# A new table of turns for the opening of a one-core attention and MLP kernel, and thirteen wide operations on other engines

## The chip, the cores and the metric

The kernel runs on one core of one Trainium2 chip. The metric is device time of one execution in microseconds, smaller is better. It is compared by the median of several runs. All engines are fed from instruction lists that are fixed when the program is built: PE (TensorE) does matmuls and transposes, DVE (VectorE), ACT (ScalarE) and POOL (GpSimd) work on tiles, and SP (SyncE) issues transfers.

## The reference, cut to what matters

```
q, k, v: [8, 8, 576, 64] fp32     w_in: [512, 2048]     w_out: [2048, 512]
q_s = softmax(q, over the 64 dims);  k_s = softmax(k, over the 576 positions)
kv  = k_s^T v                      # one 64x64 matrix for each head
x   = q_s kv                       # then laid out as 4608 tokens x 512
g   = s * relu(x @ w_in)^2 + b
out = g @ w_out                    # [4608, 512]
```

## The kernel before, in words

Eight batches (blocks of 512 tokens, and the 64 left over of each batch apart) go through two matmuls with 16 slices of the hidden dimension. For each block `t = 16 * blk + f` is a step: `step(t)` multiplies the slice f of w_in with x (12 matmuls of 512 columns into the one PSUM bank "h"), takes relu on ACT, squares and scales on DVE, and adds the slice's product with w_out to the accumulators (12 matmuls more). fp32 accuracy comes from splitting every operand into a high and a low part and multiplying high by high, high by low and low by high, so each operand costs one copy (ACT) for its high part and one subtraction (DVE) for its low part.

All weights are converted once, in the opening, by `conv_w(f)`: six operations in turn, ACT, DVE, ACT, DVE, ACT, DVE (lines 307, 311, 314, 318, 323, 326), on both halves of a slice at once (128x1024) or, for the slices in HALVES, on w_in's half ("a") and w_out's half ("b") by themselves (128x512). The attention of the first two batches is made in the opening too. `k_stream(u)` (u = 0 to 3) transposes k on PE (line 440), takes the maximum on DVE (443), the exponential on ACT (448), transposes back on PE (453) and copies the result (455, operation 4, engine by KN_ON). `kv_stream(pr)` takes the scales on DVE (408, 409), makes kv on PE (402) and scales it on DVE (420). `q_stream(u)` (u = 0 to 7) has twelve operations: 0 maximum (519), 1 subtract (522, engine by SUB_ON), 2 a small memset (526), 3 exponential (528), 4 sum (531), 5 reciprocal (533), 6 multiply (538, engine by MUL_ON), 7 transposes on PE (543), 8 copy (546, engine by QF_ON), 9 the product with kv on PE (553), 10 and 11 x's high part (559, ACT) and low part (563, DVE). `q_left` (582 to 610) does the 64 tokens left over, `k_pair` the k of the second batch. Step 0 can begin only when x of a head pair is there, and step 1 only when relu of step 0 has emptied the bank "h" and w_in's slice 1 is converted. From step 80 on the kernel multiplies by a scheme with fewer products; nothing of that is touched.

The order of the work on each engine is written into the program by a planner, `Order.run`. It holds one stream per piece of work (`conv_w`, `step`, `q_stream` and so on). The string TURNS_TAKEN holds 3557 turns, two letters each, and each names the stream whose next operation is issued. So the string fixes the order of all five instruction lists; each engine then runs its own list in that order and waits, at its head, for what the head needs. The planner's own clock has one effect left on the program: where it believes that PE is idle, `idle` (1691) puts transposes of no use into PE's list (tile "unused") until step 0, so that PE does not rest.

Below, `conv2.4` is operation 4 (counted from 0) of slice 2's conversion, `conv0b` that of w_out's half of slice 0, `q2.9` operation 9 of q_stream(2), `k3.4` operation 4 of k_stream(3), `kv1.2` operation 2 of kv_stream(1), `step0.8` the relu of step 0 (its operations 0 to 7 are its first product, 8 to 11 relu, square, high and low part, 12 to 15 its second product).

Of the kernel before, what the change touches and what calls it, by code (L numbers as in the profile page):

```python
# [26 lines left out]
def attention_moe(ctx: ExitStack, tc: tile.TileContext, q, k, v, w_in, w_out, s, b, out):  # L27
    nc = tc.nc
    B, H, S, D = q.shape
    DM, FF = w_in.shape  # L30
    DO = w_out.shape[1]
    P = 128
# [12 lines left out]
    AHEAD = min(4, FIRST)  # L45
    PAIRS = tuple((a, a + 1) for a in range(FIRST, B, 2))
    STEPS_ON_ACT = (17, 25, 26, 27, 37, 38, 40, 46, 48, 52, 53, 54, 59, 65, 75, 79)
    KN_ON = ('ACT', 'DVE', 'ACT', 'DVE')
    QF_ON = ('DVE', 'ACT', 'ACT', 'ACT', 'ACT', 'ACT', 'ACT', 'DVE')
    WARM = 20  # L50
    BEGIN = (-7.9, -6.8, 2.8, 1.8, 0.8, -0.0, -1.7, -0.6, 2.0, -3.6, -0.1, -5.5)
    SUB_ON = ('D', 'D', 'P', 'P', 'D', 'D', 'D', 'P')
    MUL_ON = ('P', 'D', 'P', 'D', 'D', 'D', 'P', 'D')
    HALVES = (0, 6, 11, 12, 13, 15)
    DUE_L = (0.5, 10.0, 12.0, 17.5)
    QF_AT_KE = (3, 4, 6)
# [70 lines left out]
    class Op:  # L127
# [8 lines left out]

    LETTERS = "abcdefghijklmnopqrstuvwxyzABCDEFGHIJKLMNOPQRSTUVWXYZ0123456789"
    TURNS_TAKEN = (
        "aaaaababaaaaabaaabaWabaWabaQaWaWabaQaWaQabaWaXaWaQabaXaRaQaWauaRaXabaXaWabaRaXaba8aRaXabaXavabaRabauaSavabaua8avaSabauabaSaYaoauaSa8aYaZaTaS"
        "aqauaWaYaZaYaTaXaWaYaTaZbcaYaWaYaZa9aTaXaZbcaXaTawaZaYaZaXa9awaYaXawavaZbcaZa9adbcawavaYadaxaZavaeaYaxaeacaZbcaYawaZbcbcacayawbcbcaye1axbdbc"  # L140
        "bda4bcaxbda4aybdbcafaxafa4aybdbcbdbcaxagbdbcagaUbcbdbeaUaybebda4beazayapbeaAbda4e2a4bdazbea4bdaAazbdbeaAa4bfazbfbeaAbfa4ahaza4ahbfbea4aiaDaU"
        "azbeaibfbeaDaAbebfbeaDaAbgbfbgaDe3aBbgaCbfbgakaDaBbfakaCa1bgbfaDaBbfaCbfbgaEbhaBbgbhaCbgaBbhajaCbhajaBbgaCbhe4a1bgaFbha1bga1aEbgbha1biaEbhbi"
        "a1bia1aGbiaEa1bibhaUalbiaFbhalaGbibha0bibha0a1aUbibja0aEaUbjaFaEbjbjaGaUbiaFaJbibjbiaJaUambjbiaJamaGbkbjbkaUaJanbkaFbjanbaa5aJaFa5aGbkarbaaK"
        "babjaJbaa5bjaKataGbjaKbkbjaKaHblbkaKblaHbkaKe5blaHbkblaIaHbkblaIbkaHblaIbkaHblbkaIe6a0bmblaIbma0asa5aIbmaNa0a1a0aLa5bma1a5aNblbma5a1blbmaVa0"
        "bmblaVbmblaLa0bnbmaNa0aNaLbna0bnaMa0bnaNaLa5bmaMbnaNbma5aLa5bnaMbma5aLbmbnaMe7boaObnboaMaOaPboaMaOaPboa2aPaVaObnboaVbnboaPaVboa2bnaVa2bnboaV"
        "bpaOaPbpboaVaObpaVaPbpe8a2a3bobpa2a3bobpa2boa2bpboa3bqbpa3a2bpbqa3a2bqa3a3bqbpbqeQeQbpbqbpbqbpbqa3bbbqa3brbbcubrbbbbbrcva2cwbra2bqa2brcxbqbr"
        "a3brbqbrbqa3brbsa3bsa6bsa7bsdgbrbsdgbrbsbrePdgdQbrbsdgePbtdQeQbtbtbseQbtdgdRdgbsbtbsdRbta6bsa7bta6bsbtbua7btbua6a7a6bua7a6a7bua6a7bta6bubta7"
        "bua6btbudgbta6budQa6bvdQbvdQbvdQbvbubvdQbubvdQbubvbubwbvdgbwbwdgdsbwdsa6bvdtcza7bwdtbva7bwdRbvbwa7dRbveea7e9bwbxe9dRbxfhdRdQbxfhefcydRfhbxdR"
        "efcBfhbwefbxbwfhefbxbwefdSbxbwfhdSbxfhbyfabyfhcCbyfibyfifhfibxbyfibxfidQbybxfadQbybxcAdhdSbzbybzdRdhbzdSbzdhdSbydhbzfbdSfibyerbzfibydhbzdSdh"
        "byerbzbAdSerbAfibAererdibAfifjbzdibAbzfjbAbzfbdTbAbzcDfjdRdTbAbBdRbBdhbBfjdTdibBdSfjdibAdTbBfcbAbBfjdTbAdifjdTdibAbBfjbCbBesdTfjbCbBesfkbCes"  # L150
        "bCdTfkesbBdhesbCfcbBfkbCdhbBdufkdUbBbCdufkbDdUdifkdvbDbCdvbDdSbCbDfkcEdSbCbDfkbCdUfdflbCbDflfkbCdUbDbEfldUbDflegdUdTflbDbEcFegbEflegflbEdieg"
        "bDbEdUegbDdwbEbDfddwflbEdUbDdicGbFbEdxbFflfmbFdxdVbFfmdVfmetbFfebEetbFbEfmbFetbEbFetbEetfmbGcHfmdTbGfmbGdTbGdVehfebGdVdUeSbGbFdVeSbGehcJbFdV"
# [235 lines left out]
    def copier(eng):  # L388
        return nc.scalar.copy if eng == "ACT" else nc.vector.tensor_copy

    def wide_op(on, part=1.0):
        return (("DVEp", 0.03 + 0.7 * part), nc.vector) if on == "D" else (("POOL", 0.1 + 1.16 * part), nc.gpsimd)
# [39 lines left out]
    def k_stream(u):  # L432
# [19 lines left out]
        for n in range(NT):  # L452
            nc.tensor.transpose(kn[:, n * P:(n + 1) * P], early[:, n * P:(n + 1) * P], ident)
        yield Op(KN_ON[u], 0.62 if KN_ON[u] == "ACT" else 0.73, due, free=[tag], gives=[f"k{u}"])
        copier(KN_ON[u])(kt, kn[:, 0:NT * P].rearrange("p (n h d) -> p h n d", n=NT, h=2))

# [51 lines left out]
    def q_stream(u):  # L508
# [10 lines left out]
        nc.vector.tensor_reduce(out=qm, in_=qt, axis=AX.X, op=ALU.max)  # L519
        on, engine = wide_op(SUB_ON[u], wide_)  # L520
        yield Op(*on, due)
# [11 lines left out]
        nc.vector.reciprocal(qs, qs)  # L533
        on, engine = wide_op(MUL_ON[u], wide_)
        yield Op(*on, due)
# [6 lines left out]
        for n in range(m):  # L542
            nc.tensor.transpose(qT[:, n * P:(n + 1) * P], qn[:, n].rearrange("p h d -> p (h d)"), ident)
        yield Op(QF_ON[u], (0.55 if QF_ON[u] == "ACT" else 0.66) * SM / S, due, free=[tag])
        qf = early[:, 0:SM] if at == "ke" else early[:, NT * P:NT * P + SM]
        copier(QF_ON[u])(qf, qT[:, 0:SM])
        yield Op("PE", 1.0 * SM / S, due, needs=[f"kvf{pr}"] + before * (bb > 0), take=[tag], free=[at])
# [1211 lines left out]
```

## Time and profile before

| | |
|---|---|
| median of 3 runs | 828.17 us (827.79 to 828.49) |
| the profiled execution | 828.27 us, of which the span is 826.5 us |
| PE busy | 817.6 us, 99% of the span |
| DVE, ACT, POOL busy | 81%, 56%, 25% of the span |
| TensorE's granted clock | full in every slice |
| DMA | 165.64 MB, mean 200 GB/s |

Busy is the time in which an engine had an instruction of the program under way. PE's matmuls are pipelined and their ends are modelled, so that a long wait shows as idle time and a short one as a larger distance between the starts of two matmuls.

### The profile page before, as it was taken

How to read it: one execution, taken by the hardware profiler on the slowest of the kernel's cores; microseconds unless marked ns; L12 is line 12 of the kernel's file. 1: busy time of each engine (PE TensorE's matmuls, PEld its weight loads, DVE VectorE, ACT ScalarE, POOL GpSimd, SP SyncE). 2: the span in 40 equal slices, each digit the busy share in tenths (PEclk: the TensorE clock that was granted, in tenths of full speed). 3: DMA queues.
4: the chain of work that ended last, by engine and by line, in shares of the span. 5: the costliest groups of instructions: out<-in, count | busy, mean ns of one | idle time of the engine just before them, and what ended most of it. 6: DMA issues, size and time to landing. Idle time of an engine off the chain costs nothing.

```text
span 826.5 us, 12888 instructions
## 1 busy us (share of the span) xinstructions
PE 817.6 (99%) x4301; PEld 676.7 (82%) x4301; DVE 673.3 (81%) x1155; ACT 463.5 (56%) x768; POOL 205.3 (25%) x206
## 2 busy tenths in 40 slices
PE   8999999999999999999999999999999999999997
PEld 7688888888888888888888888888888888888886
DVE  6999956799899996978979978699969976656883
ACT  4999964356446455564556555545447644445650
POOL 3100012212212122222222322335342005353500
PEclk9999999999999999999999999999999999999999
DMA  9999523587867666866695754789889967666314
GB/s 267 319 375 318 164 70 110 151 228 191 218 179 198 168 170 205 214 177 144 203 241 163 242 149 149 231 264 283 276 253 325 251 156 214 203 182 187 90 18 73
DMA packets 217206, 165.64 MB, mean 200 GB/s; under 512 B 91444, under 2 KB 200500, under 8 KB 217140
## 3 DMA queue, kind: packets, MB, share of 16 engines
q1 hardware_dynamic: 212116, 163.83, 68.6%
q10 hardware_dynamic: 5024, 0.98, 0.6%
q8 instruction: 34, 0.56, 0.3%
q14 instruction: 32, 0.26, 0.1%
HBM read 112.85 MB, written 52.44 MB: 200 GB/s over the span
## 4 chain that ended last, share of the span: by engine, by line
PE 96%; DVE 2%; issue 1%; ACT 0%; POOL 0%; POOLq 0%; ACTq 0%
PE acc L1548 27%; PE h L1468 26%; PE bankU L1104 11%; PE overX L1195 8%; PE bankV L1104 8%; PE overY L1195 5%; PE overZ L1195 5%; PE xp L830 2%; PE kv L402 2%; PE kT L440 1%; PE xp L553 1%; PE unused L1702 0%; PE bankU L1195 0%; DVE low L318 0%; DVE st L311 0%
## 5 line engine op out<-in xcount | busy, mean ns | idle before, releaser
L1468 PE MATMUL h<-x,w 128*128 128x512 f32 x960 | 238.2, 392 | 1.3 <-ACT r L1500 0.8
L1468 PEld LDWEIGHTS h<-x,w 128*128 128x128 f32 x960 | 177.9, 188 | 38.8 <-ACT r L1500 1.3
L1548 PE MATMUL acc<-w,gh 128*128 128x512 f32 x640 | 199.2, 392 | 0.0
L1548 PEld LDWEIGHTS acc<-w,gh 128*128 128x128 f32 x640 | 118.1, 188 | 23.5
L1548 PE MATMUL acc<-w,gl 128*128 128x512 f32 x320 | 125.1, 391 | 0.1
L1500 ACT ACTIVATE r<-h 128x512 f32<-128x512 f32 x80 | 47.9, 599 | 94.7 <-PE h L1468 94.1
L1104 PE MATMUL bankU<-w,ring 128*128 128x512 f32 x378 | 95.9, 389 | 0.0
L1104 PEld LDWEIGHTS bankU<-w,ring 128*128 128x128 f32 x378 | 70.9, 188 | 14.7
L1548 PEld LDWEIGHTS acc<-w,gl 128*128 128x128 f32 x320 | 60.1, 188 | 14.2 <-DVE gl L1527 0.9
L1104 PE MATMUL bankV<-w,ring 128*128 128x512 f32 x282 | 71.5, 389 | 0.0
L759 POOL TENSOR_TENSOR qe<-qe,qr 128x640 f32<-128x640 f32 x24 | 33.2, 1384 | 127.8 <-DVE qr L755 66.7
L1104 PEld LDWEIGHTS bankV<-w,ring 128*128 128x128 f32 x282 | 52.9, 188 | 11.0
L1514 DVE SCALAR_TENSOR_TENSOR h<-h,sb,r 128x512 f32<-128x512 f32 x47 | 35.3, 752 | 18.3 <-ACT r L1500 18.0
L742 POOL TENSOR_TENSOR area<-area,qm 128x640 f32<-128x640 f32 x24 | 31.2, 1300 | 74.3 <-DVE qm L740 45.4
L1516 ACT ACTIVATE gh<-h,sb 128x512 fp32r<-128x512 f32 x47 | 32.4, 690 | 28.6 <-DVE h L1514 28.5
L1195 PE MATMUL overX<-w,w 128*128 128x512 f32 (+1 forms) x177 | 40.5, 384 | 0.0
L1195 PEld LDWEIGHTS overX<-w,w 128*128 128x128 f32 x177 | 32.7, 188 | 6.5
L1518 DVE SCALAR_TENSOR_TENSOR gl<-h,sb,gh 128x512 fp32r<-128x512 f32 x47 | 34.7, 738 | 3.4 <-ACT gh L1516 3.2
L1510 DVE TENSOR_TENSOR gl<-r,gh 128x512 fp32r<-128x512 f32 x23 | 17.5, 762 | 15.6 <-ACT gh L1508 15.5
L927 DVE TENSOR_TENSOR S<-S 128x128 f32<-128x128 f32 x64 | 26.7, 418 | 0.7
L1195 PE MATMUL overZ<-gh,w 128*128 128x512 f32 x88 | 27.1, 389 | 0.0
L927 DVE TENSOR_TENSOR Z<-Z 128x128 f32<-128x128 f32 x64 | 25.2, 394 | 1.0
(329 smaller groups left out, 1524.1 us busy)
## 6 DMA issues: line engine op xcount, KB each, us to landing
ring<-aset SPq DMA_DIRECT2D x55, 512.0 KB, 4.0
w<-wset SPq DMA_DIRECT2D x80, 256.0 KB, 3.9
st<-in_moe_w_in_dram SPq DMA_DIRECT2D x16, 512.0 KB, 7.8
st<-in_moe_w_out_dram SPq DMA_DIRECT2D x16, 512.0 KB, 8.6
wset<-Z SPq DMA_DIRECT2D x32, 256.0 KB, 3.9
turned<-area SPq DMA_DIRECT2D x24, 320.0 KB, 3.6
qe<-turned SPq DMA_DIRECT2D x48, 160.0 KB, 3.5
area<-in_v_dram SPq DMA_DIRECT2D x56, 128.0 KB, 3.8
```

What stands on the lines that cost most here:

```text
L742: nc.gpsimd.tensor_tensor(out=qt, in0=qt, in1=bc(qm, [P, 2, NT, D]), op=ALU.subtract)
L759: nc.gpsimd.tensor_tensor(out=qe_, in0=qe_, in1=qr, op=ALU.mult)
L927: eng.tensor_tensor(out=o, in0=x, in1=y, op=op)
L1104: nc.tensor.matmul(out_, w[:, a, c * P:(c + 1) * P], slot(k, c)[:, b_], start=k in (0, 1, 3) and n == 0, stop=n == 5, skip_group_check=True)
L1195: nc.tensor.matmul(out_, w[:, l], g[m][:, cols], start=k not in (2, 4) and p == begin_ and n == 0, stop=p == end_ and n == 2, skip_group_c ...
L1468: nc.tensor.matmul(hp_, w[:, j, c, :], x[:, c, :], start=(c == 0 and i == 0), stop=(c == NP - 1 and i == 2))
L1500: nc.scalar.activation(r, hp_, AF.Relu)
L1510: nc.vector.tensor_tensor(out=gl, in0=r, in1=gh.bitcast(F32), op=ALU.subtract)
L1514: nc.vector.scalar_tensor_tensor(out=hp_, in0=hp_, scalar=s_col, in1=r, op0=ALU.mult, op1=ALU.mult)
L1516: nc.scalar.activation(gh, hp_, AF.Identity, bias=b_col)
L1518: nc.vector.scalar_tensor_tensor(out=gl, in0=hp_, scalar=b_col, in1=gh.bitcast(F32), op0=ALU.add, op1=ALU.subtract)
L1548: nc.tensor.matmul(acc[blk, j // 2][:, j % 2], g[:, js], w_, start=(f == 0 and i == 0), stop=(f == NFC - 1 and i == 2))
```

## The change

Four tuples of engines change, thirteen entries in all. The copies of k 1 and 3 go from DVE to ACT; the copy of q 0 goes from DVE to ACT and that of q 3 from ACT to DVE; the subtractions of q 0, 1, 5 and 6 go from DVE to POOL and those of q 2 and 7 from POOL to DVE; the multiplications of q 1, 3 and 5 go from DVE to POOL. The first 770 turns of the table are new (up to about step 21); the other 2787 are the same, in the same places.

```diff
-    KN_ON = ('ACT', 'DVE', 'ACT', 'DVE')
-    QF_ON = ('DVE', 'ACT', 'ACT', 'ACT', 'ACT', 'ACT', 'ACT', 'DVE')
+    KN_ON = ('ACT', 'ACT', 'ACT', 'ACT')
+    QF_ON = ('ACT', 'ACT', 'ACT', 'DVE', 'ACT', 'ACT', 'ACT', 'DVE')
-    SUB_ON = ('D', 'D', 'P', 'P', 'D', 'D', 'D', 'P')
-    MUL_ON = ('P', 'D', 'P', 'D', 'D', 'D', 'P', 'D')
+    SUB_ON = ('P', 'P', 'D', 'P', 'D', 'P', 'P', 'D')
+    MUL_ON = ('P', 'P', 'P', 'P', 'D', 'P', 'P', 'D')
     TURNS_TAKEN = (
-        "aaaaababaaaaabaaabaWabaWabaQaWaWabaQaWaQabaWaXaWaQabaXaRaQaWauaRaXabaXaWabaRaXaba8aRaXabaXavabaRabauaSavabaua8avaSabauabaSaYaoauaSa8aYaZaTaS"
+        "aaaaaaabaaabababababaWaWaWaQaQaWaQaQauaRaXaWauaWaXaRaQaXaWauaXaRauaWaXauaua8aXavavaRaSaRaSa8ababababababababaWavaYaZa8avaXaYaYaSaSaSavaYaTaT"
...
```

Read turn by turn, the two tables give these lists up to step 1 (POOL's to about step 6).

```
DVE before: q0.0 q0.1 k0.1 q0.4 q0.5 q1.0 q1.1 k1.1 q0.8 q1.4 kv0.0 q1.5 q1.6 k1.4 conv0a.1 conv0b.1 k2.1 conv0a.3 q2.0 kv0.2
            q3.0 conv0a.5 k3.1 q2.4 q2.5 q0.11 kv1.0 q3.4 k3.4 q3.5 q3.6 conv1.1 q1.11 conv0b.3 kv1.2 conv1.3 conv0b.5 conv2.1
            q2.11 q3.11 scalars.1 conv1.5 conv3.1 step0.9 q_left0.0 conv2.3 step0.11
DVE after:  q0.0 k0.1 q1.0 q0.4 conv0a.1 q0.5 k1.1 conv0a.3 q1.4 conv0a.5 kv0.0 q1.5 conv0b.1 k2.1 q2.0 q3.0 kv0.2 conv0b.3 q2.1
            k3.1 q2.4 q0.11 q2.5 kv1.0 q3.4 q3.5 conv0b.5 conv1.1 q1.11 kv1.2 q3.8 conv2.1 conv1.3 q2.11 q3.11 scalars.1 conv1.5
            q_left0.0 step0.9 conv2.3 step0.11
ACT before: q0.3 k0.2 k0.4 conv0a.0 q1.3 k1.2 conv0b.0 conv0a.2 conv0b.2 k2.2 conv0a.4 k2.4 q2.3 q0.10 k3.2 q3.3 q1.8 conv1.0
            q1.10 q2.8 conv1.2 q3.8 conv0b.4 conv2.0 q2.10 q3.10 conv1.4 conv3.0 step0.8 conv2.2 step0.10
ACT after:  q0.3 k0.2 conv0a.0 k0.4 conv0a.2 q1.3 k1.2 conv0a.4 conv0b.0 k1.4 q0.8 conv0b.2 k2.2 k2.4 conv0b.4 q2.3 q0.10 k3.2
            q3.3 q1.8 k3.4 conv1.0 q1.10 q2.8 conv2.0 conv1.2 q2.10 q3.10 conv1.4 conv2.2 step0.8 conv3.0 step0.10
PE before:  ... k3.3 step0.1 q1.9 q2.7 kv1.1 q3.7 step0.2 step0.3 q2.9 q3.9 scalars.0 step0.4 to step0.7 step1.0
PE after:   ... k3.3 q1.9 q2.7 kv1.1 q3.7 step0.1 q2.9 scalars.0 q3.9 step0.2 to step0.7 step1.0
POOL before: q0.2 q0.6 q1.2 q2.1 q2.2 q3.1 q3.2 q2.6 q_left0.1 q_left0.2 q_left0.6 q5.2 q4.2 ...
POOL after:  q0.1 q0.2 q1.1 q1.2 q0.6 q1.6 q2.2 q3.1 q3.2 q2.6 q3.6 q_left0.1 q_left0.2 q_left0.6 q5.1 ...
```

DVE's lists go on, to the last conversion of slice 5:

```
DVE before: step0.9 q_left0.0 conv2.3 step0.11 conv3.3 conv2.5 k_pair2.0 k_pair2.1 step1.8 conv3.5 q_left0.4 q_left0.5
            conv4.1 conv5.1 step2.5 conv4.3 conv5.3 step2.7 conv4.5 conv7.1 step3.5 conv5.5
DVE after:  step0.9 conv2.3 step0.11 conv3.1 conv2.5 q_left1.0 conv3.3 q_left0.4 q_left0.5 k_pair2.0 step1.8 k_pair2.1
            conv4.1 conv3.5 step2.5 k_pair2.3 conv4.3 step2.7 conv6a.1 conv5.1 conv4.5 step3.5 conv5.3 conv6a.3
            conv7.1 step3.7 q5.0 conv5.5
```

Further on, in PE's list after, the last quarter of a step's second product stands behind the next step's first product more often (step 0's behind step 2's first), and `k_pair` and the q of the second batch come earlier. On SP, the load of the second batch's k and the first half of slice 6 go ahead of slice 4's second half, and the eight `a_copies` (copies of converted weights to DRAM, 0.75 MB each, read from step 80 on) move from between the loads of slices 6 to 15 to behind them. An activation of one element, which stood ahead of the first exponential on ACT (line 1627), moves to the middle of the opening.

## Rows read from the trace of the kernel before

**Rows 1.** Busy time by stretch: time, length, PE, PEld, DVE, ACT, POOL, clock, DMA, GB/s
```profile
0.00:33.00 33.00, 28.57 (x273) 22.89 (x273) 25.36 (x47) 21.52 (x36) 7.83 (x25) 1.00 0.99 295
33.00:57.00 24.00, 23.90 (x107) 19.09 (x107) 23.13 (x31) 22.76 (x32) 2.63 (x5) 1.00 1.04 344
110.00:150.00 40.00, 40.00 (x218) 33.16 (x217) 21.31 (x43) 18.11 (x30) 7.71 (x13) 1.00 0.30 86
```
**Rows 2.** Waits of PE and of its weight loads: total us, times, longest
```profile
PE h L1468 <- ACT r L1500: 0.8, 1, 0.8
PEld acc L1548 <- DVE gl L1527: 0.9, 2, 0.5
```
**Rows 3.** PE in order of time: start us, us, instruction, count, idle before
```profile
14.09 1.04 PE L1702 MATMUL unused<-ident 128*128 128x128 f32 x8
...
25.30 1.39 PE L402 MATMUL kv<-raw 128*64 128x64 f32 x40
...
32.96 3.01 PE L1468 MATMUL h<-x,w 128*128 128x512 f32 x12 [0.78 <-ACT r L1500]
35.80 0.61 PE L1548 MATMUL acc<-w,gh 128*128 128x512 f32 x2
36.52 0.50 PE L1548 MATMUL acc<-w,gl 128*128 128x512 f32 x1
...
56.55 2.88 PE L1468 MATMUL h<-x,w 128*128 128x512 f32 x12
```
**Rows 4.** DVE in order of time, 26 to 53 us
```profile
26.56 0.67 DVE L318 SCALAR_TENSOR_TENSOR low<-st,low 128x512 uint32<-128x512 uint32 x1
27.16 0.58 DVE L420 TENSOR_TENSOR kvf<-kv,z 64x128 f32<-64x128 f32 x2
...
30.23 1.29 DVE L563 TENSOR_TENSOR x<-xp,x 128x512 fp32r<-128x512 f32 x2
...
51.05 1.23 DVE L326 TENSOR_TENSOR w<-low,w 128x1024 fp32r<-128x1024 f32 x1 [0.19 <-ACT w L323]
```
**Rows 5.** ACT in order of time, 31 to 33 us
```profile
31.27 1.14 ACT L307 ACTIVATE low<-st 128x1024 int32<-128x1024 uint32 x1
32.31 0.59 ACT L1500 ACTIVATE r<-h 128x512 f32<-128x512 f32 x1
```
**Rows 6.** DVE and POOL in order of time, where they meet
```profile
10.20 1.19 DVE L522 TENSOR_TENSOR area<-area,qm 128x512 f32<-128x512 f32 x1
...
35.37 1.10 DVE L1527 SCALAR_TENSOR_TENSOR gl<-r,sb,gh 128x512 fp32r<-128x512 f32 x1
```
**Rows 7.** POOL in order of time
```profile
9.80 1.05 POOL L538 TENSOR_TENSOR qe<-qe,qs 128x512 f32<-128x512 f32 x1 [5.96 <-ACT early L448]
...
34.40 1.53 POOL L584 TENSOR_TENSOR area<-area,qml 128x256 f32<-128x256 f32 x1 [11.37 <-DVE qml L582]
...
42.71 0.90 POOL L599 TENSOR_TENSOR ql<-ql,qsl 128x256 f32<-128x256 f32 x1 [6.74 <-DVE qsl L596]
```
**Rows 8.** Groups of instructions, 0 to 130 us: count | busy us, mean ns | idle before
```profile
L318 DVE SCALAR_TENSOR_TENSOR low<-st,low 128x1024 uint32<-128x1024 uint32 x10 | 12.1, 1218 | 0.9 <-ACT st L314 0.8
...
L1523 DVE SCALAR_TENSOR_TENSOR r<-r,sb 128x512 f32<-128x512 f32 x9 | 6.7, 744 | 0.9 <-ACT r L1500 0.9
...
L538 DVE TENSOR_TENSOR qe<-qe,qs 128x512 f32<-128x512 f32 x5 | 3.5, 692 | 0.2
...
L1627 ACT ACT_TABLE_LOAD x1 | 1.3, 1283 | 3.2 <-issue 3.2
```
**Rows 9.** All engines in order of time: slice 4's transfer and its conversion
```profile
22.95 0.33 SPq L293 DMA_DIRECT2D st<-in_moe_w_out_dram  x1
...
40.56 2.17 ACT L307 ACTIVATE low<-st 128x1024 int32<-128x1024 uint32 x2
```
**Rows 10.** DVE in order of time: the last operation on the late q
```profile
166.45 0.82 DVE L776 TENSOR_TENSOR spare<-qe,spare 128x640 fp32r<-128x640 f32 x1
```
**Rows 11.** PE in order of time: the product that uses it
```profile
171.69 0.96 PE L830 MATMUL xp<-spare 128*128 128x320 f32 x6
```

More of the change, by code (lines that the diff above doesn't have):

```diff
@@ L138, in attention_moe @@
     TURNS_TAKEN = (
-        "aaaaababaaaaabaaabaWabaWabaQaWaWabaQaWaQabaWaXaWaQabaXaRaQaWauaRaXabaXaWabaRaXaba8aRaXabaXavabaRabauaSavabaua8avaSabauabaSaYaoauaSa8aYaZaTaS"
-        "aqauaWaYaZaYaTaXaWaYaTaZbcaYaWaYaZa9aTaXaZbcaXaTawaZaYaZaXa9awaYaXawavaZbcaZa9adbcawavaYadaxaZavaeaYaxaeacaZbcaYawaZbcbcacayawbcbcaye1axbdbc"
-        "bda4bcaxbda4aybdbcafaxafa4aybdbcbdbcaxagbdbcagaUbcbdbeaUaybebda4beazayapbeaAbda4e2a4bdazbea4bdaAazbdbeaAa4bfazbfbeaAbfa4ahaza4ahbfbea4aiaDaU"
-        "azbeaibfbeaDaAbebfbeaDaAbgbfbgaDe3aBbgaCbfbgakaDaBbfakaCa1bgbfaDaBbfaCbfbgaEbhaBbgbhaCbgaBbhajaCbhajaBbgaCbhe4a1bgaFbha1bga1aEbgbha1biaEbhbi"
@@ L143, in attention_moe @@
[L143 to L146, printed above, removed]
@@ L147, in attention_moe @@
-        "a3brbqbrbqa3brbsa3bsa6bsa7bsdgbrbsdgbrbsbrePdgdQbrbsdgePbtdQeQbtbtbseQbtdgdRdgbsbtbsdRbta6bsa7bta6bsbtbua7btbua6a7a6bua7a6a7bua6a7bta6bubta7"
-        "bua6btbudgbta6budQa6bvdQbvdQbvdQbvbubvdQbubvdQbubvbubwbvdgbwbwdgdsbwdsa6bvdtcza7bwdtbva7bwdRbvbwa7dRbveea7e9bwbxe9dRbxfhdRdQbxfhefcydRfhbxdR"
-        "efcBfhbwefbxbwfhefbxbwefdSbxbwfhdSbxfhbyfabyfhcCbyfibyfifhfibxbyfibxfidQbybxfadQbybxcAdhdSbzbybzdRdhbzdSbzdhdSbydhbzfbdSfibyerbzfibydhbzdSdh"
+        "aaaaaaabaaabababababaWaWaWaQaQaWaQaQauaRaXaWauaWaXaRaQaXaWauaXaRauaWaXauaua8aXavavaRaSaRaSa8ababababababababaWavaYaZa8avaXaYaYaSaSaSavaYaTaT"
@@ new lines, in attention_moe @@
+        "aYaWaWaXaTaZaZaZaXaWaYa9aZaZavbcaTaXaYaTawaXaYaYaxa9awaXaZa9aZbcawaZaYacaZaYaZaxawawaYaZacbcbcbcbcbcbcaxbcawa4bcaxbdbdbdbdabababaoaeabaqaday"
+        "bcbcaxayaxa5a4a4bdaybda4bdbdazaya4a4aUbdbcbcbcbebebebebcaybeadafapagafagaeaUazayaBazbebeaAbdbdbdaUbfbdbfbfbfa4aUazazbeaBaAazaBbfaAbfaDbfa4aU"
+        "bebeaAaBaDbfa1bgbgbgbebebgaBaAaAaabgaUbgaEaEaBaUbfbfbhbfbhbhbhbfa1a5a5a1aDbgbgaEaEa1aCaDbhaEaUaUbha4bhaDbgbgbibibibibgbgbaaiahaiahaka1aEa0bh"
+        "aCa1aFa5a4aCaFbaaCaDaFbiaCa4a0aFa1biaGaGbibhbhbhbha1bjbjbjbja0biaCbiaGbjaFa0aGakarajanalanajatamamasalbibibkbkbkbkbibiaVbjbjaFbjbaa0aVa1aGaH"
@@ new lines, in attention_moe @@
+        "baaKbkbjbjbja1aVbjblblblblaGaHaHaKbkaVa0a5a0a1aJbkaHbkaJaJa1blaKa5aJaJbkblblaKaKblaHaHaKa0a0aVbmbmbma5bmbkbkbkblbla5aLaIaLaIaJaIbmaNaIa2a3a2"
+        "a2bmaLa5bmbmaVaNa3a3bma3a2a2aVbnblblbnbnbna5a5bnaIaNaVaVbmbmbobobobobmbma0bba3a2aIbnbnaPaLbnaNaLaLaPaNa0aMboa0aMa3a3bnbnbpbpbpbna3bnbpaMaMbb"
+        "bbaNbba3boboaOboaMboaMaOa2a3bpbpa3a3aPbpaOaObobqbobobqa2bqbqboaOaPbpbpaOa2aPbqa2brbrbrbrbpbpbqbqa2bqa2bqbpbqbpbqbqbqcvcxe5cucwa7a6e1e2aPa7dg"
+        "a6brbrbrbrbsbsbsbrdga6a6eQa6a6a6a6eQbrbsbrbra6bsbrdRdQdgbsdQePbsbtbseQdgbtbtbtbsbsbsbsdgdQbta7a7a6btbta7a6dQa6bta7a7btdQbubububuePdge4dga7a7"
@@ L150, in attention_moe @@
+        "btbtbtbta7bubudgbudgbudsa7a7dRbvbvbubububvbvbudReedsdQdRbvbvdQbvdtdtbvbwbwbwbwbwbvbvbvbvbxbxbxefbwdRfhfhdRdRbwbwfhbxdQcye3cze7dQefcBfhbwefbx"
+        "bwfhefbxbwefdSbxbwfhdSbxfhbyfadRbyfhcCbyfibyfifheQfibxbyfibxfidQbybxfae9e9dQbybxcAe8dhdSbzbybzdRdhbzdSbzdhdSbydhbzfbdSfibyerbzfibydhbzdSdhe6"
         "byerbzbAdSerbAfibAererdibAfifjbzdibAbzfjbAbzfbdTbAbzcDfjdRdTbAbBdRbBdhbBfjdTdibBdSfjdibAdTbBfcbAbBfjdTbAdifjdTdibAbBfjbCbBesdTfjbCbBesfkbCes"
```

## The prediction

> **What bounds the kernel now.** I read the busy time by stretch first. From 57 us on PE has no idle time that the view shows (40.00 of 40.00 us between 110 and 150, for one) and the clock stands at full in all three stretches, so nothing that DVE, ACT or POOL do there can shorten the kernel unless it removes matmuls, and the change removes none. Before 33 us PE is busy for 28.57 of 33 us, and part of that is the transposes of no use; DVE has 25.36 and the DMA engines 0.99 of it. Between 33 and 57 us PE has lost 0.10 us, while DVE is busy 23.13 and ACT 22.76 of 24 us [rows 1]. So the kernel is a dense row of matmuls behind a start-up of some 33 us, and the next two views say where the row begins and where it tears.
>
> The waits of PE give the places: 0.8 us in one wait of step 1's first product for the relu of step 0, and 0.9 us in two waits of a weight load for a low part of g, which DVE makes [rows 2]. In order of time the first is at 32.96: from there on PE runs through. The second is the one at 36.52: two matmuls begin from 35.80 on and the third at 36.52; twelve matmuls take 2.84 us there (32.96 to 35.80), 0.24 each, so 0.25 us is lost [rows 3]. I take the same for its twin near 54 us.
>
> So the change can gain in two ways only: an earlier 32.96, and fewer tears behind it. 0.2% of this time, 1.7 us, is about what a measurement of this kernel tells from no change; "the same" below means 826.5 to 829.8.
>
> **The chain that ends at 32.96, before.** The kv of heads 2 and 3 runs on PE from 25.30 and is done at 26.69. Its scaling on DVE begins only at 27.16, since DVE is in a conversion from 26.56 to 27.23 [rows 3, 4]. The products for x 2 and x 3 wait for it. Their low parts are made on DVE from 30.23 to 31.52 [rows 4]; step 0 needs them for its last matmuls and is done at about 32.2. Its relu starts on ACT at 32.31, behind a conversion from 31.27 to 32.41 (the next instruction starts a little before the end of the last, here 1.04 us after its start) [rows 5]. The relu ends at 32.90, and step 1 begins at 32.96.
>
> **The chain after, by hand on the new lists.** Durations are those of the rows; I go from the old times and move what the lists move.
> - The half conversion ahead of the scaling (conv0b.3) now stands behind the scaling of heads 0 and 1, some 8 us earlier. DVE's list between is shorter by the copy of k 3 (no shorter than 0.69) and the multiplication of q 3 (0.69) [rows 8]. The scaling starts when kv is done: 26.75, a gain of 0.4. The copy of q 3 that DVE now makes (0.69 by the nearest row) runs beside the product of q 2, so it hides; without that cover it costs 0.3.
> - The low parts of x 2 and x 3 stand behind conv1.3 (1.22 [rows 8]), which waits for conv1.2 on ACT. ACT has behind q 1's copy the copy of k 3, conv1.0, x 1's high part, q 2's copy, conv2.0 and conv1.2: three copies of about 0.6 and three long ones of 1.04 to 1.1, some 5 us from 23.5, so conv1.2 ends at 28.5. conv1.3 then runs to 29.7, x 2's low part from 29.6 and x 3's from 30.2 to 30.9: 0.6 earlier than before.
> - The relu is ready at 31.6, but ACT has conv1.4 (from 29.7) and conv2.2 ahead of it, 1.04 and 1.1 us; it begins at 31.8, 0.5 earlier. Step 1 begins at 32.45. First term: **-0.5 us**.
>
> **The tears behind it.** The first came from POOL. Its subtraction for the left-over tokens took 1.53 us at 34.40 against 0.90 for its like at 42.71, and the low part of g that DVE began at 35.37, while POOL was at work until 35.93, took 1.10 us where the square of the same size takes 0.74 [rows 6 to 8]. In the new list the left-over maximum stands ahead of the square of step 0, so that POOL's operation begins just before the square is ready, and the square is held for up to 0.9 us; g's low part then ends at 35.8, and PE wants it at about 35.7 (32.45 and 2.84, then two matmuls). The old tears go, **-0.5 us**; this one leaves **+0.1**. Slice 2 must now be converted 0.7 us earlier relative to PE's work, since the last quarter of step 0's second product stands behind step 2's first product; DVE's four operations behind the square (conv2.3, g's low part, conv3.1 and conv2.5: 1.2, 0.7, 0.7 and 1.2) end near 37.6, and PE is there at 37.5: **+0.1**.
>
> Sum: -0.5 - 0.5 + 0.1 + 0.1 = -0.8. On the profiled execution's own time, 828.27 (its span of 826.5 and 1.77 around it), that is 827.5; it lies 0.1 above the median, so the forecast against the median is **827.4**.
>
> **Parts at nothing, and what covers them.**
> - The transposes of no use: eight of them ended when k 2's transposes began, 1.04 us long [rows 3]. Their number follows the planner's clock and may change either way; between -0.5 and +0.5, taken 0.
> - The table load ahead of the first activation, 1.28 us [rows 8]: it began before the one-element activation had its operand, so it does not wait; between 0 and +1.3 on a path that has a microsecond to spare before q 0's transposes, taken 0.
> - Slice 4's second half is loaded behind 0.5 MB of slice 6 and 0.58 MB of k. At 344 GB/s [rows 1] that is 3.1 us. It was issued at 22.95 and is converted from 40.56 [rows 9]: the 3.1 us lie in those 17.6. Without that cover, +3 us at most.
> - The eight copies to DRAM, 6 MB, move behind the loads, into a stretch with a DMA share of 0.30 [rows 1]. Two stand on SP between the late q's turn to DRAM and its way back, with a k and a q: 2.4 MB, some 7 us. The way back was issued with room, and its last DVE operation ends at 167.27, 4.4 us before PE uses it [rows 10, 11]. Taken 0; 0 to +2.
> - The three operations of the second batch that go to POOL: there PE waits for none of them. Below nothing they could give 0.25, the tear near 54 us, which is in the sum.
>
> **The rivals.**
> 1. *DVE was the whole bound of the opening.* Ahead of step 0's square DVE loses two copies of k, the copy of q 0, two subtractions and two multiplications (seven at 0.69, one of the subtractions with 0.5 of waiting) and gains two of 0.69: 0.69 x 5 + 0.5 = 4.0 us [rows 6, 8]. ACT gains two copies, 1.2 us. If the start moves by the middle between my 0.5 and the 2.8 that is left, some 1.7, and the tears bring 0.3 as in the sum, the kernel gains 2.0: **826.2**. For it: DVE and ACT are almost without gaps from 33 us on, and every conversion made early shortens that too. Against: DVE has 7.6 us without work before 33 us, so it waits on the chain as often as the chain on it.
> 2. *POOL takes back what DVE gave.* A two-operand operation on DVE beside one on POOL took 1.19 us against 0.69 [rows 6 to 8]: 0.5 lost. Five operations more on POOL give DVE 3.5 us and may cost it 2.5, and those ahead of the scaling of heads 2 and 3 stand on the chain; one meeting there takes back the whole first term. Then the tears alone remain, -0.3, and a second meeting takes these too: about **828.1**. The Trainium skill, Perfetto Trace Analysis, Optimizing Scalar/DVE Operations, warns of just this: the two engines share a read port, so moving work between them might not help. By that sentence alone the time would be the old one; the trace agrees that they meet, with the 1.19 us [rows 6], and says nothing on how often the new lists will.
> 3. *The conversions come late: slower.* Before, slice 5's conversion ended at 52.28, 4.3 us ahead of PE's use at 56.55 [rows 3, 4]. In the new list about 3 us more work of DVE stand ahead of its end (halves of slices 3 and 6, step 3's low part, a maximum of the second batch), and PE is there 1.5 us of its own work sooner. That leaves nothing. PE then runs at DVE's pace between slices 3 and 5, where DVE is busy 96% [rows 1]. Each meeting with POOL costs 0.5 more, and four POOL operations lie there: -0.8 + 0.5 + 4 x 0.5 = +1.7, **829.9**. It decides where conv5.5 ends against step 5's first matmul: every 0.1 us that it is later is 0.1 us of time.
> 4. *The table does not reach the chip's order.* The lists are in program order and every engine follows its own; I give this nothing.
>
> **How the numbers follow.** The forecast, 826.6 to 828.4, has 0.50; rival 1 0.24; rival 2 0.11; rival 3 0.15. The forecast and rival 2 are the same within 0.2%, though the edge of the forecast touches 826.5, so faster has 0.26, same 0.58, slower 0.16. The range goes from 825.7 (rival 1 with the fills half a microsecond shorter) to 829.6 (rival 3 with three meetings), and leaves out the tails of both.
>
> **What would show it.** In the waits of PE after: step 1's first product near 32.4 and still behind the relu; no wait for g's low part over 0.3 us; new small waits of a weight load of "h" for slices 2 to 5. DVE's first scaling of heads 2 and 3 directly behind kv. A DVE operation of two SBUF operands of over 1 us beside each new POOL operation. I would be wrong if step 1 began before 31.5 (rival 1) or after 33, if a weight load of h waits for DVE by more than 0.5 us near step 5 (rival 3), or if PE waits anywhere behind 60 us, which no row gives reason for.

## The result, and the profile after

The kernel after takes **839.36 us** in the median of four runs (839.17 to 840.51), the kernel before 827.98 beside it: a ratio of **1.014** (95% interval 1.0123 to 1.0158), so 11.4 us slower. The forecast was 827.4, with a range up to 829.6. The profiled execution of after took 840.51 us, its span 838.8, 12.3 us more than the span of before.

Where do the 12.3 us lie? From step 14 on both kernels run the second products of the steps at the same place in PE's list, so their ends can be compared, after minus before: steps 14 to 16 are 1.9 to 2.1 us late, step 17 2.6, step 18 9.7, steps 19 to 24 9.0, step 26 12.3, and so it stays to the end of the kernel. So there are three places: some 2 us up to 128 us, some 7 us at step 18, and 3.3 us at step 26.

The busy time by stretch shows all three, the last two plainly (columns as in [rows 1]):

```profile
0.00:33.00 33.00, 27.92 (x273) 22.83 (x273) 22.21 (x42) 22.26 (x36) 11.59 (x27) 1.00 1.00 293
33.00:57.00 24.00, 23.77 (x108) 19.58 (x108) 23.85 (x34) 21.91 (x30) 5.58 (x8) 1.00 0.99 313
75.00:90.00 15.00, 14.12 (x63) 10.57 (x63) 13.74 (x24) 10.88 (x21) 1.13 (x1) 1.00 1.08 327
145.00:150.00 5.00, 3.15 (x16) 2.33 (x14) 0.00 (x0) 0.41 (x1) 0.00 (x0) 1.00 0.55 86
150.00:155.00 5.00, 1.85 (x4) 1.49 (x5) 3.04 (x4) 1.74 (x4) 1.46 (x2) 0.52 0.10 18
155.00:160.00 5.00, 5.00 (x19) 4.01 (x18) 1.06 (x2) 0.86 (x2) 0.00 (x0) 0.79 0.00 0
200.00:205.00 5.00, 3.52 (x17) 2.59 (x15) 3.52 (x7) 3.17 (x6) 0.93 (x2) 1.00 0.90 260
```

The opening did what the change says: DVE has 22.21 us of the first 33 where it had 25.36, POOL 11.59 where it had 7.83 [rows 1]. But between 145 and 155 us PE stands for 5.0 us, and in the first half of that stretch DVE, ACT and POOL do almost nothing (0.00, 0.41 and 0.00 of 5 us). With all of them idle at once, something outside them is awaited. The waits of PE name where it surfaces (answering [rows 2]):

```profile
PE acc L1548 <- DVE gl L1518: 5.0, 1, 5.0
...
PE acc L1548 <- ACT gh L1508: 1.5, 1, 1.5
PE acc L1548 <- DVE gl L1510: 1.0, 2, 0.7
PE h L1468 <- ACT r L1500: 0.8, 1, 0.8
```

**The place at 153 us.** PE waits for step 18's low part of g (L1518). DVE, in order of time, shows why that is late, and it is not the operation itself:

```profile
150.88 1.56 DVE L687 TENSOR_TENSOR area<-area,misc 128x640 f32<-128x640 f32 x2 [6.19 <-DMA misc<-maxima]
152.35 0.74 DVE L1518 SCALAR_TENSOR_TENSOR gl<-h,sb,gh 128x512 fp32r<-128x512 f32 x1
```

The head of DVE's list is L687, which subtracts maxima that go to DRAM and come back spread over the partitions. It waits 6.19 us for them, and the low part, whose operands have long been there, stands behind. So the next view is SP's list, which issues both ways of the maxima (L679 out, L683 back):

```profile
121.11 0.72 SPq L890 DMA_DIRECT2D aset<-w  x1
140.45 0.36 SPq L352 DMA_DIRECT2D xleft<-misc  x1
140.85 0.47 SPq L1569 DMA_DIRECT2D out_dram<-o  x1
141.42 0.38 SPq L679 DMA_DIRECT2D maxima<-sb  x1
141.84 1.34 SPq L889 DMA_DIRECT2D aset<-w  x2
143.22 0.50 SPq L890 DMA_DIRECT2D aset<-w  x1
146.99 0.33 SPq L683 DMA_DIRECT2D misc<-maxima  x1
```

Before, the same two, and the subtraction that uses them on DVE, were:

```profile
134.83 0.33 SPq L679 DMA_DIRECT2D maxima<-sb  x1
137.67 0.33 SPq L683 DMA_DIRECT2D misc<-maxima  x1
```
```profile
149.36 1.55 DVE L687 TENSOR_TENSOR area<-area,misc 128x640 f32<-128x640 f32 x2
```

Two things stand in their way. First, SP issues nothing from 121.8 to 140.45: at its head stands L352, a store of left-over rows that waits for ACT's copy L345. DVE's last work on the maxima ended at 137.30, and they leave only at 141.42. Second, between out (141.42) and back (146.99) lie 5.6 us instead of 2.8, with a copy of weights to DRAM (L889, L890, 0.75 MB) issued right behind the way out; what that copy costs, copies_early and store_ahead show below. The waits of SP add up all stays at L352, after and before:

```profile
SPq L352 <- ACT misc L345: 50.5, 4, 18.5
```
```profile
SPq L352 <- ACT misc L345: 17.4, 3, 11.5
```

The store is written in the function that makes ACT's copy, so the turn that orders it is a turn of ACT (shortened; ... marks what is left out):

```
def keep_left(u, x):                       # called in ACT's turn
    ...
    nc.scalar.copy(t[:, i], x)             # L345
    ...
    if len(there) == 2 and pr < NP:
        store_left(pr)                     # L352: nc.sync.dma_start, on SP
```

In SP's list it stands wherever ACT's turn stands in the table. Read as lists of engines, as I read the two tables, it is not on SP at all.

The 5.0 us are not all. PE in order of time:

```profile
146.06 1.64 PE L1468 MATMUL h<-x,w 128*128 128x512 f32 x6
147.53 0.62 PE L1548 MATMUL acc<-w,gh 128*128 128x512 f32 x2
153.15 0.80 PE L1548 MATMUL acc<-w,gl 128*128 128x512 f32 x1 [5.00 <-DVE gl L1518]
153.75 1.05 PE L1548 MATMUL acc<-w,gh 128*128 128x512 f32 x2
...
156.31 1.91 PE L1468 MATMUL h<-x,w 128*128 128x512 f32 x6
```

The granted clock stood at 1.00 up to 150 us, was 0.52 in the stretch with the idle time and 0.79 in the next. Behind the wait two matmuls take 1.05 us where two took 0.62; the seven from 153.15 to 156.31 take 3.16 us, against about 1.6 at 0.23 each. With the six that follow (1.91 instead of 1.64) that is some 1.8 us lost at the lower of the two levels (1.2 of 2.4 GHz): 5.0 + 1.8 are nearly the 7 us of step 18.

**The place at 204 us** has the same form, with ACT's list in the chain as well:

```profile
200.58 2.88 PE L1468 MATMUL h<-x,w 128*128 128x512 f32 x12
204.94 0.73 PE L1548 MATMUL acc<-w,gh 128*128 128x512 f32 x2 [1.48 <-ACT gh L1508]
```
```profile
202.30 0.74 ACT L729 ACTIVATE kalt<-kalt 128x640 f32<-128x640 f32 x1 [1.83 <-DVE kalt L687]
202.95 0.80 ACT L1506 ACTIVATE r<-r,sb 128x512 f32<-128x512 f32 x1
```

DVE's L687 for the next pair waits 2.05 us for its maxima until 201.44, ACT's exponential L729 for DVE, and ACT's two operations of the step behind it. **At 75 us** it is a load of k; SP's head is again L352, from 50.5 us until 68.44, and DVE waits 2.15 us for the load with step 6's square behind it:

```profile
68.44 0.38 SPq L352 DMA_DIRECT2D xleft<-misc  x1
68.87 0.46 SPq L293 DMA_DIRECT2D st<-in_moe_w_out_dram  x1
69.43 1.46 SPq L375 DMA_DIRECT2D area<-in_k_dram  x1
```
```profile
75.83 0.69 DVE L621 TENSOR_TENSOR misc<-area 128x512 f32<-128x512 f32 x1 [2.15 <-DMA area<-in_k_dram]
```

### The profile page after: what moved, and what is told of

Its sections match the earlier page's. It is cut to its first block, busy times and chain, and to the rows that moved or that the text cites. A ratio compares the mean times of both kernels' runs of the same rounds, so it can differ in the third digit from the quotient of the medians.

```text
span 838.8 us, 12899 instructions
## 1 busy us (share of the span) xinstructions
PE 820.6 (98%) x4302; PEld 677.4 (81%) x4302; DVE 671.4 (80%) x1148; ACT 462.7 (55%) x770; POOL 212.0 (25%) x211
## 4 chain that ended last, share of the span: by engine, by line
PE 88%; DMA 6%; DVE 3%; ACT 1%; issue 1%; SPq 1%; ACTq 0%; DVEq 0%
PE acc L1548 23%; PE h L1468 23%; PE bankU L1104 10%; PE overX L1195 8%; PE bankV L1104 8%; PE overY L1195 5%; PE overZ L1195 5%; PE kv L402 2%; PE xp L830 2%; DMA misc<-maxima 1%; DMA st<-in_moe_w_out_dram 1%; DMA raw<-in_k_dram 1%; DMA area<-in_k_dram 1%; DMA area<-in_q_dram 1%; DMA maxima<-sb 1%
## 5 line engine op out<-in xcount | busy, mean ns | idle before, releaser
L1516 ACT ACTIVATE gh<-h,sb 128x512 fp32r<-128x512 f32 x47 | 32.4, 690 | 29.7 <-DVE h L1514 29.6
L1518 DVE SCALAR_TENSOR_TENSOR gl<-h,sb,gh 128x512 fp32r<-128x512 f32 x47 | 34.6, 736 | 1.8 <-ACT gh L1516 1.7
```

The costliest lines, as they stand in the source:

```text
L1516: nc.scalar.activation(gh, hp_, AF.Identity, bias=b_col)
L1518: nc.vector.scalar_tensor_tensor(out=gl, in0=hp_, scalar=b_col, in1=gh.bitcast(F32), op0=ALU.add, op1=ALU.subtract)
```

## The experiments

The table of turns is edited in all but two; the diffs show its turns decoded, in the order of one engine's list. The medians of before beside these runs lie between 827.95 and 828.58. What the expectations call the ninth pair is the pair of k 8 and 9.

**Engines or order?** Two kernels swap the four tuples and the table crosswise.

```diff
# old_table_new_engines: before, with
+ KN_ON, QF_ON, SUB_ON, MUL_ON of after
# new_table_old_engines: after, with
+ KN_ON, QF_ON, SUB_ON, MUL_ON of before
```

> The table of before with the four new tuples of engines. Theory T (the loss lies in the order of the lists of turns, which puts waits for late transfers ahead of a step's products): 827 to 831, since the order is the old one. Rival E (the thirteen operations cost it, GpSimd holding VectorE or ACT too full): 835 or more.

> The table of after with the four old tuples of engines. Theory T: the late waits stay, 837 to 842, with the 5 us wait of TensorE near 150 us still there. Rival E: 831 or less.

Measured: 829.87 (1.0024, interval 1.0014 to 1.0033) and 843.73 (1.0190, 1.0170 to 1.0209). The new engines with the old table cost 1.9 us, with a new wait of 0.8 us for POOL at 65 us; with the new table they save 4.4 (843.73 is even above theory T's range, with a wait of 5.2 us near 150 us, as T says). So the table costs the 11 us, and the engines are worth something only in the order planned for them.

**The new opening with the old order behind it.**

```diff
# h540
  turns 0 to 539 of after
- turns 540 to 769 of after
+ what is left, in the order of before
```

> After up to turn 540 (step 14, about 110 us), then everything that is left in the order of before. Theory T: the waits at 150 and 200 us go (9.4 us), those at 75 to 110 us stay (3.4 us) and the opening's 0.6 us gain stays: about 830. Rival I (the lateness is inherited from the opening, whose loads and copies went to DRAM in another order): 835 or more.

Measured: 828.91 (1.0011, 1.0002 to 1.0021), with PE busy for 35.00 of 35 us from 130 to 165 and 65.00 of 65 from 165 to 230. Nothing of the 10 us at steps 18 and 26 is inherited: they belong to the order behind turn 540.

**The copies, the store, and both.**

```diff
# copies_early (SP)
  a_copies 0, 1
+ a_copies 3, 2, 6, 7, 5
  store of left rows (L352), store of out, maxima out
- a_copies 3, and 2, 6, 7, 5 further on
  maxima back
# store_ahead (SP)
+ store of out, maxima out
  store of left rows (L352)
- store of out, maxima out
# copies_store: both
```

> After, with the five copies of converted weights to DRAM that stand behind 140 us in SP's list (slices 6/7, 4/5, 12/13, 14/15, 10/11) moved ahead, into the stretch from 122 to 140 us in which SP only waits. Theory C (these copies make the maxima of the ninth pair and the later transfers late): the maxima's way out and back is 3 us shorter, so the wait of 5 us shrinks to about 2, and the wait at 195 to 210 us (3 us) goes: about 833. Rival L (the lists' order alone: the store of the left rows that waits for ACT in SP's list, and VectorE's k_late ahead of step 18's low part): at most 1 us less, 838 to 840.

> copies_early, and in SP's list the store of an output tile and the maxima's way to DRAM moved ahead of the store of left rows that waits for ACT's copy until 140.4 us. The maxima can then leave at 137.3 instead of 141.3. Theory S (that wait in SP's list is the rest of the lateness): the maxima are back near 145.4 instead of 149.4, the wait of 3.6 us shrinks under 0.5 and the clock does not fall: 829.5 to 831. Rival (the way through DRAM is slow wherever it stands): less than 1.5 us gained, 833.5 or more.

> After, with only the second of the two edits of copies_store: the store of an output tile and the maxima's way to DRAM moved ahead of the store of left rows; the five copies of weights stay late. Theory S (each edit takes its own wait): the wait of 5 us near 150 us goes with the clock's fall behind it, some 6 us, and the wait at 195 to 210 us (3 us) stays: 833 to 834.5. Rival C (the late copies are behind both waits): 2 to 3 us gained, 836.5 to 837.5, with some 3 us of the wait near 150 us left.

Measured: copies_early 835.10 (1.0088, 1.0073 to 1.0103), store_ahead 835.37 (1.0085, 1.0070 to 1.0099), both together **829.24** (1.0010, 1.0001 to 1.0019). In copies_early the wait at 204 us is gone, as theory C says, but that at 150 us is 3.6 us and not 2, with the clock still falling; in store_ahead it is 2.2 us without a fall of the clock, and the later one stays. store_ahead gains some 1 to 2 us less than theory S gave it. The maxima's whole way, from the issue out to the landing back, takes 7.6 us before, 9.5 in after and 8.1 in copies_early, 10.7 in store_ahead and 8.3 in both together: the late copies cost that way 1.4 us where the store stands ahead of the maxima and 2.4 where it stands behind them. Of the 5.6 us between out and back, 3.9 are left in copies_early, so the copy is not the whole of the difference to the 2.8 of before. The kernels do not have the same runs of before beside them. Taken against the before beside each, after stands 11.4 us above it, copies_early 7.2, store_ahead 7.2 and both together 0.7. In both together SP and the waits look like this (SP in order of time, then PE's waits from the largest):

```profile
136.45 0.33 SPq L679 DMA_DIRECT2D maxima<-sb  x1
139.56 0.36 SPq L352 DMA_DIRECT2D xleft<-misc  x1
141.21 0.33 SPq L683 DMA_DIRECT2D misc<-maxima  x1
```
```profile
PE unused L1702 <- POOL ident masks.py:199: 2.3, 1, 2.3
PE h L1468 <- ACT r L1500: 1.2, 2, 1.1
```

The 2.3 us stand ahead of the first thing PE does, in each of these kernels, and the 1.2 end at 32.64; nothing behind 33 us is left above 0.3.

**The wait or the list it stands in?**

```diff
# low_first (DVE)
- L687 of k 8 and 9
  low part of step 18
  ... second operation and low part of step 19
+ L687 of k 8 and 9, then (ACT, POOL) its exponentials
```

> After, with VectorE's two subtractions of the ninth pair's maxima (L687, which wait for the maxima's way through DRAM) moved behind the low parts of steps 18 and 19, and what hangs on them (the exponentials of that pair, one store of left rows that takes the same buffer) behind that; nothing else moves, the copies and SP's list are those of after. Theory T (what stops TensorE is that a list in order holds a step's low part behind the wait): the 5 us wait near 150 us and the low clock behind it go, 6 to 7 us, 832 to 834; the waits at 75 to 110 and 195 to 210 us stay. Rival D (the transfers' lateness itself binds): TensorE waits for the same maxima a little later, at the pair's own products, and the time is 837 or more.

Measured: 834.23 (1.0069, 1.0055 to 1.0083). The wait at 150 us is gone with the maxima as late as in after, so theory T holds there: what stopped PE was the place in the list. But 2 us of the 7 come back where the late transfers are met next. PE waits there twice, and the clock falls:

```profile
190.00:195.00 5.00, 3.01 (x7) 2.12 (x8) 3.86 (x9) 2.38 (x5) 0.33 (x1) 0.74 0.82 201
```
```profile
190.61 0.73 PE L1548 MATMUL acc<-w,gh 128*128 128x512 f32 x2 [1.06 <-ACT gh L1508]
192.72 0.80 PE L1548 MATMUL acc<-w,gl 128*128 128x512 f32 x1 [1.37 <-DVE gl L1510]
193.31 1.05 PE L1548 MATMUL acc<-w,gh 128*128 128x512 f32 x2
```

**The late copies alone, in the old order.**

```diff
# before_copies_late: before (SP)
- a_copies 2, 3, 5, 6, 7 between 53 and 102 us
+ the same behind the transfers that they follow in after
```

> Before, with one edit: the five copies of weights that after has late stand late here too, behind the same transfers of SP's list as in after. Theory C (late copies delay the transfers that the later lists wait for, whatever the opening): the wait at 195 to 210 us comes, 2 to 3 us, and near 150 us at most 0.5, since the maxima have 7 us of slack there: 830 to 831.5. Rival (they only add to a lateness that the new order made): 828 to 828.5.

Measured: 830.38 (1.0033, 1.0021 to 1.0045), and a wide spread, 829.16 to 833.70. The row of 190 to 195 us is PE's only loss behind 130 us in this profiled execution, which is the fastest of the ten: the steps behind it end 1.5 us later than those ahead of it, compared with before. Between 150 and 155 us there was slack enough.

```profile
190.00:195.00 5.00, 4.07 (x18) 2.75 (x16) 4.87 (x9) 3.83 (x6) 1.66 (x3) 1.00 1.02 239
```

**The place at 75 us.**

```diff
# k_load_ahead (SP); stores_behind_all: the same in copies_store
+ load of slice 12's second half, load of k 6 and 7
  store of left rows (L352)
- load of slice 12's second half, load of k 6 and 7
```

> After, with one load of weights (slice 12's second half) and the load of the fourth pair's k moved ahead of the store of left rows at which SP's list stands from 50 to 68 us. Theory S (that store holds the load, VectorE waits 2.2 us for it at 73.7 to 75.8 us with step 6's second activation behind it): the waits of TensorE at 78, 79 and 86.6 us go, 1.3 to 1.9 us, while the later ones stay: 837 to 838.5. Rival (the load is late for its own wait, the product that frees its buffer): 839 to 841.

> copies_store with the edit of k_load_ahead. Theory S: its 829.2 less the 1.3 to 1.9 us at 75 to 90 us, 827.3 to 828; the opening's 1 us gain is then left nearly whole. Rival: 829 or more.

Measured: k_load_ahead 839.55 (1.0141, 1.0124 to 1.0157), runs from 836.93 to 840.17; the profiled one is the fastest. Its trace shows the load issued at 65.12 instead of 69.43 and DVE no longer waiting for it, and PE busy for 54.84 of the 55 us from 75 to 130 (53.98 in after); but the median has not moved and lies in the rival's range, so that by itself this run is inconclusive. stores_behind_all: **827.83** (0.9999, 0.9990 to 1.0008). With the three edits of SP's list the whole 11.4 us are back. The stretches in which after lost time have no idle PE left:

```profile
75.00:90.00 15.00, 15.00 (x72) 12.47 (x71) 14.13 (x27) 12.64 (x25) 1.14 (x1) 1.00 0.83 247
150.00:155.00 5.00, 5.00 (x24) 4.14 (x23) 3.82 (x8) 2.60 (x4) 1.10 (x2) 1.00 0.61 180
200.00:205.00 5.00, 5.00 (x24) 4.14 (x23) 4.97 (x8) 2.94 (x5) 1.33 (x3) 1.00 0.88 229
```

**Can the opening's gain be had alone?** Five kernels take less of the new table.

```diff
# h180, h300: as h540, from turn 180 and 300
# h180e, h220e: from turn 180 and 220, and
- SUB_ON, MUL_ON of after for q 5 to 7
+ SUB_ON, MUL_ON of before for q 5 to 7
# h180t: h180e, with (ACT, DVE)
- first two operations of slice 7's conversion
  step 3's relu (ACT), step 3's square (DVE)
+ first two operations of slice 7's conversion
# and (PE) the transposes xpl behind three more products
```

> After up to turn 180 (the opening's streams and step 1), then everything left in the order of before; the engines are those of after. If the opening of the new table is worth what the trace of after shows up to 60 us (0.6 us), and no new wait comes behind it: 827.3. Rival (the old order behind the new opening is late for slices 2 to 5, as the engines' swap alone was): 829 or more.

> As h180, with the new order kept up to turn 300 (step 6). The gains at 33 to 60 us (0.7 us) are kept too, and the waits at 75 to 110 us are those of before: 827.0 to 827.5. Rival (the waits at 75 to 90 us are an outcome of the loads' order up to there): 828.5 or more, with the waits still at 75 to 90 us.

> h180 with the engines of before for the streams of q 5 to 7 (their subtractions and multiplications), which run behind 40 us in the old order; the streams up to q 3 keep the new ones. The wait of 1.0 us at 65 us, for GpSimd's part of one of these, goes, and those at 45 and 53 us shrink: 0 to 40 us gives 1.4 us less waiting than before, the rest as before: 826.8 to 827.3. Rival (the gain to 40 us is taken back behind it, by slices 3 to 5): 828.3 or more.

> As h180e, with the new order kept up to turn 220 (step 4). If the new order of VectorE for slices 3 and 4 is worth its 0.4 us at 40 to 60 us, 826.5 to 827; if the hand-over to the old order is late, as in h300, 829 or more.

> h180e with two operations of slice 7's conversion (which wait for their transfer until 48.1 us) behind step 3's activation and its second operation on ACT and VectorE, and the transposes of left rows behind three more products in TensorE's list. If the opening's gain was lost to these waits (1.0 us at 45.7, 0.7 us at 53.9), 826.6 to 827.3; if the transfers of the weights themselves set slices 4 to 7, the waits move to the next conversion: 828 or more.

Measured: h180 829.47 (1.0014, 1.0005 to 1.0023), h300 832.32 (1.0052, 1.0040 to 1.0065), h180e 828.35 (1.0000, 0.9991 to 1.0008), h220e 830.33 (1.0023, 1.0013 to 1.0032), h180t 828.07 (1.0001, 0.9991 to 1.0010). All five lie in the range of their rival. h180's wait of 0.8 us for POOL at 65 us goes with the old engines of q 5 to 7, as expected. What h180e gains up to 40 us it loses at 45.7 and 53.9 us, where conversions stand for their transfers. In h180t these waits are gone, but step 1 began at 33.05 in its profiled execution, as late as in before: no gain was there to keep, and the later start alone may have covered the waits. In h180e it had begun at 31.41 with the same first 180 turns, so one profiled execution does not give the opening's gain. h300 has a new wait of 2.2 us at 68.3 us, for ACT's copy L345. None of the five beats before, and no version here does; the best, stores_behind_all, cannot be told from it.

## Why the prediction was wrong

- **The step that failed** is the one on the copies: "The eight copies to DRAM, 6 MB, move behind the loads, into a stretch with a DMA share of 0.30 ... Taken 0; 0 to +2". Five late copies cost 839.36 - 835.10 = 4.3 us in after and 2.3 us in the old order. Most of the 4.3 is the place at 204 us, where after loses 3.3 us and copies_early nothing. I had placed the hazard at the late q and taken a mean DMA share for room. The maxima's way out and back, with one copy issued between its two legs, is a chain of two latencies, and 7 us of slack on DVE (issued back at 137.67 and landed at 142.40, used at 149.36, before) was used up.
- **The step that was missing** is the store L352. I followed SP's loads and copies and left out the DMA that rides in a turn of ACT. Each kernel taken against the before beside it, moving the maxima ahead of it is worth 6.5 us with the copies early (7.2 above before, then 0.7) and 4.1 with the copies late (11.4, then 7.2). The third edit, at 75 us, brings some 1 us (0.7 above before, then 0.3 below); the two ratios' intervals overlap, so that the times do not show this one. The traces do: step 1 begins at 32.64 and 32.66 in the two, and step 14 ends 1.55 us earlier with the edit.
- **"or if PE waits anywhere behind 60 us, which no row gives reason for"**: it does, at 78, 153 and 204 us. The sentence that "nothing that DVE, ACT or POOL do there can shorten the kernel" was right and misleading, because they can lengthen it: 40.00 of 40.00 us busy [rows 1] says nothing on how much slack stands behind each wait.
- **The first term, -0.5.** In the profiled execution of after, step 1 began at 33.23, not at 32.45; 0.27 later than before [rows 3] (PE, then DVE, then ACT).

```profile
24.57 1.39 PE L402 MATMUL kv<-raw 128*64 128x64 f32 x40
...
33.23 3.02 PE L1468 MATMUL h<-x,w 128*128 128x512 f32 x12 [0.81 <-ACT r L1500]
36.08 0.62 PE L1548 MATMUL acc<-w,gh 128*128 128x512 f32 x2
36.54 0.39 PE L1548 MATMUL acc<-w,gl 128*128 128x512 f32 x1
```
```profile
26.06 0.69 DVE L563 TENSOR_TENSOR x<-xp,x 128x512 fp32r<-128x512 f32 x1 [0.46 <-ACT x L559]
26.67 0.58 DVE L420 TENSOR_TENSOR kvf<-kv,z 64x128 f32<-64x128 f32 x2
...
29.34 1.22 DVE L318 SCALAR_TENSOR_TENSOR low<-st,low 128x1024 uint32<-128x1024 uint32 x1 [0.60 <-ACT st L314]
...
33.88 1.64 DVE L318 SCALAR_TENSOR_TENSOR low<-st,low 128x1024 uint32<-128x1024 uint32 x1
```
```profile
27.11 1.14 ACT L307 ACTIVATE low<-st 128x1024 int32<-128x1024 uint32 x1 [0.60 <-DMA st<-in_moe_w_out_dram]
```

  The scaling of heads 2 and 3 came at 26.67, where the hand chain had 26.75 (27.16 before [rows 4]), but that is luck: kv was done at 25.96, and the scaling stood 0.7 us behind it in DVE's list, behind x 1's low part, which waited for ACT. conv1.3 ended at 30.56 and not at 29.7: ACT stood 0.60 us at a conversion whose weights had not landed, and DVE 0.60 us behind ACT. My chain counted ACT's operations and no transfer. The same omission as with SP, in small.

  One execution does not settle this term. Seven other kernels here have the same opening (copies_early, store_ahead, copies_store, stores_behind_all, low_first, k_load_ahead, h540), and in their profiled executions step 1 began between 32.62 and 33.02. In five of them no wait for those weights shows, conv1.3 ends at 29.7 as by hand, and step 1 begins at 32.62 to 32.66, within 0.2 of the hand chain. But the old opening scatters too: step 1 began at 32.51 in before_copies_late. So a gain of 0.5 is neither shown nor excluded, and a wait for the weights of up to 0.6 is as large as the term itself.
- **The tears, -0.5 + 0.1 + 0.1.** The first is gone: the third matmul of step 0's second product begins 0.46 us behind the first (36.08, 36.54), where it was 0.72 [rows 3]. POOL now meets conv2.3 instead, 1.64 us at 33.88 against 1.22; ACT's conv2.4 waits 0.73 us for it, PE does not. The old twin was taken too large: before, its two matmuls begin at 53.52 and the third at 54.12, so at 0.23 each it lost 0.14 and not 0.25, and the two tears were worth 0.4.
- **Rival 3** had the right place and no price: conv5.5 ended at 54.49 and step 5's first matmul began at 54.50, straight behind the matmul before it. Nothing was left, as it said, and nothing lost. (The range's upper edge, this rival with three meetings, comes to 829.4 by its own terms, not 829.6; the outcome is far outside either.)
- **Rival 2 and the second batch's operations**, taken at 0: with the old order the new engines cost 1.9 us, with one wait of 0.8 for POOL in the trace. The tables are not independent of the engines, which I had treated as separate terms.
- The opening as a whole: with SP's three places mended, the new table stands 0.1 us below before, with an interval from -0.8 to +0.7. The forecast of -0.8 is at its edge; no gain is shown. In its profiled execution the later steps end 0.55 us earlier than in before, 0.30 of it already at the start of step 1, which is inside the scatter above.

## What to carry to other kernels

When an order is rewritten, read the new order of every queue, the one that issues transfers first, and put each instruction under the engine that executes it, not under the turn that emits it. A full engine row says that there was enough slack, not how much: for each transfer that moves, take the row where it landed and the row that used it, and subtract. A list in order turns the lateness of one transfer into lateness for all that stands behind it, through four lists here: ACT's copy, SP's store, DVE's subtraction, PE's product.

## What the runs showed of the hardware

SP's track was empty for 18 us at a time (121.8 to 140.45) and SP's list was still what held the maxima back: its waits show that, its busy time does not. The Trainium skill, DMA: Bandwidth & Descriptors, Issuing engines are not separate DMA queues, says that starting DMAs from several engines saves only the time of the sequencer, which is usually small beside the transfer. That is about the number of issuing engines, and no run here moves a transfer to another engine's list. What the runs show is the place within one list: it was worth 6.5 us (copies_early against copies_store) with the same transfers. Issuing L352 from ACT's own queue, which would take it out of SP's list, was not tried.

The granted clock fell behind PE's idle stretches of 5.0 us (after) and 3.6 us (copies_early, 0.56 from 150 to 155 us), and did not behind the 2.2 us of store_ahead (1.00). The length of one wait does not settle it: in low_first it fell behind two waits of 1.06 and 1.37 us, 2.1 us apart (0.74 from 190 to 195 us; two matmuls then took 1.05 us), and in after it stayed at 1.00 from 200 to 210 us, behind waits of 1.48 and 0.67 us. A wait can thus cost more than its length, some 1.8 us more in after.
